# The forward loop of a recurrent attention kernel: unit work moved between the projections and the waits of the chain

## The chip, the cores and the metric

The kernel runs on one core of one Trainium2 chip. The metric is the device time of a whole execution in microseconds (us). The kernel before takes 5009.69 us (median of three runs, 5001.88 to 5017.44).

## The reference

A layer with a memory-augmented recurrent attention (A) and a gated feed-forward (B) is run forward and backward. The outputs are the layer's result and nine gradients, in bf16. Only the forward recurrence matters here:

```python
for s in range(n_seg):                       # 64 segments of 32 tokens
    xs = x[:, s * seg_len:(s + 1) * seg_len, :].copy()
    h = jnp.concatenate([mem, xs], axis=1)   # 8 memory rows + 32 tokens, 640 wide
    q = jnp.einsum('btd,dhe->bhte', h, Wq)   # 32 heads of 128
    k = jnp.einsum('btd,dhe->bhte', h, Wk)
    v = jnp.einsum('btd,dhe->bhte', h, Wv)
    scores = jnp.einsum('bhqe,bhke->bhqk', q, k) * scale
    scores = jnp.where(mask[None, None], scores, -1000000000.0)
    p = _softmax(scores, axis=-1)
    o = jnp.einsum('bhqk,bhke->bhqe', p, v)
    o = jnp.einsum('bhte,hed->btd', o, Wo)
    mem = o[:, :M, :].copy()                 # the next segment's memory
    outs.append(o[:, M:, :])
```

## The kernel before, in words

The program is a row of phases on one core. The function `recurrence` (phase 3) is the forward loop; `chain(t, gap)` writes one step of it, for t from 0 to 63. A step has two kinds of work.

The chain is what the next step needs: the eight memory rows. With `hx` (memory rows and the rows of tokens that ride along, turned) it projects K, Q and V in halves of 512 columns (`half` and `packed_half`, L306), turns the memory rows' keys and queries by a product with a selection matrix (L314), copies them out (L521 into `kT`, L530 into `qmT`), and puts the memory rows of V into `vt` by eight small VectorE copies (L539). Then come the scores of the memory rows (L544, copied to `sTm` at L546), a transpose (L554), the softmax (maximum L556, subtraction L558, exp L560, sum L562, reciprocal L564, scaling L566 into `Pm`), a transpose of `Pm` (L571) with its two ScalarE copies into `PTm` (L574), the product with `vt` (L580) and two VectorE copies into `oTm` (L582, L583), the output projection (`packed_out`, L325), the fold of its two halves (`fold_add`: ScalarE copy L334 into `fup`, VectorE sums L336 into `fsum`), the fold's turn (L352), and the cast into the next `hx` (L597).

The unit work is the attention of the tokens. Three segments are one tile `tl`, and a unit is four heads (of eight groups, `qd`) of a tile. In step t the units of the tile before are handled: three when t mod 3 is 0 or 1, two when it is 2. A unit goes through these functions: `ld` (loads of q or v, SP queue), `turn_q` (four transposes L632, ScalarE copy L634), `scores` (L644 to L649), `soft` (VectorE maximum L658 and scaling L660; four ScalarE exps L664 with their sums), `norm` (VectorE reciprocal L674, GpSimd multiply L675, store L676), `turn_p` (transposes L683, VectorE copy L684), and in the step after `pv` (products L703 and L710, ScalarE copies L705 and L712, stores L706 on ScalarE's queue and L713 on GpSimd's). Beside it, keys of the tile after next are loaded (`ld_k`) and turned (`kprep`, L615, ScalarE copy L617). `ride` (L495) and `oride` (L694) are GpSimd copies that put token rows into `hx` and `oTm`.

What is put where is written out by hand: `chain` calls `gap(name)` at nine places (W0, W1, W2 among the projections; G1 after `sTm`; G2 after `Pm`; G3 after `PTm`; G4 before the output projection; G5 after the fold's sums; G6 after `hx`), and `FILL` lists the unit functions of each. After the filling, `gap` adds one or two matmuls that nobody reads (`WARM`, L734) in G2 to G5. At the end `in_order` (L275) ties each instruction to the one written before it on its engine, so every engine runs its instructions in the order of the text; a waiting instruction holds all behind it on its engine. The unit work's tiles in PSUM share one tag of five banks, the chain has three banks of its own (`bA`, `bB`, `bC`).

Of the kernel before, what the change touches and what calls it, by code (L numbers as in the profile page):

```python
# [16 lines left out]
P = 128  # L17
# [356 lines left out]
def phase3_Afwd(k, W4, Wv, Wk_):  # L374
    nc, tc = k.nc, k.tc
    D, DC, S, H, HD, T = k.D, k.DC, k.S, k.H, k.HD, k.T
    Wq = W4.tile([P, DC, HD], BF16, name="Wq", tag="w2")
    Wo = W4.tile([P, H, D], BF16, name="Wo", tag="w3")
    with tc.tile_pool(name="ast", bufs=1) as st:
        kTs = [st.tile([P, H, 120], BF16, name=f"kT{i}") for i in range(2)]  # L380

        vt = st.tile([104, HD // 2], BF16, name="vt")
        hxs = [st.tile([P, DC, 32], BF16, name=f"hx{i}") for i in range(2)]
        qTs = [st.tile([P, 4, P], BF16, name=f"xqT{i}") for i in range(2)]
        xPs = [st.tile([120, 4, P], BF16, name=f"xP{i}") for i in range(3)]
        PTs = [st.tile([120, 4, P], BF16, name=f"xPT{i}") for i in range(2)]
        oTm = st.tile([P, H, 32], BF16, name="oTm")
        first_part(k, Wv, Wk_, Wq, Wo, kTs, vt, hxs, qTs + xPs + PTs + [oTm])
        recurrence(k, Wv, Wk_, Wq, Wo, kTs, vt, hxs, qTs, xPs, PTs, oTm)
    return Wo  # L390
# [62 lines left out]
def recurrence(k, Wv, Wk_, Wq, Wo, kTs, vt, hxs, qTs, xPs, PTs, oTm):  # L453
    nc, tc = k.nc, k.tc
    D, DC, S, H, HD, T = k.D, k.DC, k.S, k.H, k.HD, k.T
    with tc.tile_pool(name="achain", bufs=1) as ch, \
# [3 lines left out]
        bA, bB, bC = [psm.tile([P, 512], F32, name=f"bank{i}") for i in range(3)]  # L460
        pm = bA
        rides = {}
        WARM = dict(G2=1, G3=1, G4=2, G5=1)

        def ride_ld(t):
            x0 = k.NB0 + 24 * t
            b, sub = t // 4, t % 4
# [29 lines left out]
        def chain(t, gap):  # L497
# [72 lines left out]
            for a in range(2):  # L570
                nc.tensor.transpose(ps3[64 * a:64 * a + 40, :], Pm[:, a, :], k.ident[:], tile_position=(0, 64 * a))  # L571
            PTm = ch.tile([104, 8, 16], BF16, name="PTm", tag="fsum")
            for a in range(2):
                nc.scalar.copy(PTm[64 * a:64 * a + 40].rearrange("p q h -> p (q h)"), ps3[64 * a:64 * a + 40])  # L574
            gap("G3")
            poms = [bview(b, P, 16, 8) for b in (bC, bB)]
            for j in range(16):
# [2 lines left out]
                    nc.tensor.matmul(poms[a][:, j, :], vt[p0:p0 + 40, j * P:(j + 1) * P], PTm[p0:p0 + 40, :, j],  # L580
                                     start=True, stop=True, tile_position=(p0, 0))
            nc.vector.tensor_copy(oTm[:, 0:16, 0:8], poms[0])  # L582
            nc.vector.tensor_copy(oTm[:, 16:32, 0:8], poms[1])  # L583
            dump(sv, k.QVS[t // 4, :, :, t % 4, 1])
            if t + 1 == T:
                gap("G4")
# [20 lines left out]
            k.load_x(kr, 0, k.x_src(tl, "k", c0, c0 + 512), nc.sync)  # L607
            uu["kr", tl, qd] = kr

        def kprep(tl, qd):  # L610
            ns, nm, nx, n = k.geo(tl)
            kr = uu.pop(("kr", tl, qd))
            pt = ps.tile([P, 4, nx], BF16, name="kpt", tag="x", bufs=5)
            for j in range(4):
                nc.tensor.transpose(pt[:, j, :], kr[0:nx, j * P:(j + 1) * P], k.ident[0:nx, 0:nx])  # L615
            dst = kTs[tl % 2][:, qd * 4:qd * 4 + 4, 0:n].rearrange("p h (s c) -> p h s c", c=40)[:, :, :, 8:40]
            nc.scalar.copy(dst, pt[:].rearrange("p h (s c) -> p h s c", c=32))  # L617

        def ld(w, tl, qd, eng=nc.sync):
            nm = k.geo(tl)[1]  # L620
# [6 lines left out]
        def turn_q(tl, qd):  # L627
            n = k.geo(tl)[3]
            r = uu.pop(("q", tl, qd))
            pt = ps.tile([P, 4, n], BF16, name="qpt", tag="x", bufs=5)  # L630
            for j in range(4):
                nc.tensor.transpose(pt[:, j, :], r[0:n, j * P:(j + 1) * P], k.ident[0:n, 0:n])  # L632
            qT = qTs[qd % 2]
            nc.scalar.copy(qT[:, :, 0:n], pt[:])  # L634

        def scores(tl, qd):
            ns, nm, nx, n = k.geo(tl)
            h0 = qd * 4
            kT = kTs[tl % 2]
            qT = qTs[qd % 2]  # L640
            mb = (k.mask3 if ns == 3 else k.mask1)[:]
            sp = ps.tile([P, 4, n], F32, name="xsp", tag="x", bufs=5)
            mb = bass.AP(tensor=mb.tensor, offset=mb.offset, ap=[list(mb.ap[0]), [0, 4], list(mb.ap[1])])
            nc.tensor.matmul(sp[:], k.ident[0:n, :], mb, start=True, stop=False, skip_group_check=True)  # L644
            for j in range(4):
                kv = kT[:, h0 + j, 0:n].rearrange("p (s c) -> p s c", c=40)
                nc.tensor.matmul(sp[:, j, nx:n], qT[:, j, :], kv[:, :, 0:8], start=False, stop=True,
                                 skip_group_check=True)
                nc.tensor.matmul(sp[:, j, 0:nx], qT[:, j, :], kv[:, :, 8:40], start=False, stop=True,  # L649
                                 skip_group_check=True)  # L650
            uu["s", tl, qd] = sp

        def soft(tl, qd):
            n = k.geo(tl)[3]
            h0 = qd * 4
            sp = uu.pop(("s", tl, qd))
            mx = fl.tile([120, 4], F32, name="xmx", tag="xmx", bufs=2)
            nc.vector.reduce_max(mx[0:n], sp[0:n], axis=AX.X)  # L658
            nmx = fl.tile([120, 4], F32, name="xnm", tag="xnm", bufs=2)
            nc.vector.tensor_scalar(nmx[0:n], mx[0:n], -k.scale, None, op0=ALU.mult)  # L660
            Pb = xPs[qd % 3]
            Z = fl.tile([120, 4], F32, name="xZ", tag="xZ", bufs=2)
            for j in range(4):
                nc.scalar.activation(Pb[0:n, j, 0:n], sp[0:n, j, :], ACT.Exp, bias=nmx[0:n, j:j + 1], scale=k.scale,  # L664
                                     accum_out=Z[0:n, j:j + 1])
            rz = fl.tile([120, 4], F32, name="xrz", tag="xrz", bufs=2)
            uu["z", tl, qd] = Z, rz

        def norm(tl, qd, eng=nc.gpsimd, q=nc.gpsimd):
            n = k.geo(tl)[3]  # L670
            h0 = qd * 4
            Pb = xPs[qd % 3]
            Z, rz = uu.pop(("z", tl, qd))
            nc.vector.reciprocal(rz[0:n], Z[0:n])  # L674
            eng.tensor_tensor(Pb[0:n, :, 0:n], Pb[0:n, :, 0:n], bc_last(rz[0:n], n), ALU.mult)  # L675
            q.dma_start(k.PR[tl][:, h0:h0 + 4, :], Pb[0:n])  # L676
# [16 lines left out]
            if 0 <= t - k.OT0 < k.NO:  # L693
                nc.gpsimd.tensor_copy(oTm[:, :, 8:32], uu.pop(("o", t))[:])  # L694

        def pv(tl, qd, q=nc.gpsimd):
            n = k.geo(tl)[3]
            c0 = qd * 512
            v = uu.pop(("v", tl, qd))
            if 4 * tl < k.NO:  # L700
                pt = ps.tile([P, 4, 96], F32, name="xot", tag="x", bufs=5)
                for j in range(4):
                    nc.tensor.matmul(pt[:, j, :], v[0:n, j * P:(j + 1) * P], PTs[qd % 2][0:n, j, 0:96], start=True, stop=True)  # L703
                ot = fl.tile([P, 4, 4, 24], BF16, name="xoT", tag="xoT", bufs=2)
                nc.scalar.copy(ot[:].rearrange("p c h t -> p h c t"), pt[:].rearrange("p h (c t) -> p h c t", t=24))  # L705
                nc.scalar.dma_start(k.OTX[4 * tl:4 * tl + 4, :, 4 * qd:4 * qd + 4, :].rearrange("c p h t -> p c (h t)"),  # L706
                                    ot[:].rearrange("p c h t -> p c (h t)"))
            po = ps.tile([P, 512], F32, name="xpo", tag="x", bufs=5)
            for j in range(4):
                nc.tensor.matmul(po[:, j * P:(j + 1) * P], PTs[qd % 2][0:n, j, :], v[0:n, j * P:(j + 1) * P],  # L710
                                 start=True, stop=True)
            nc.scalar.copy(v[0:n], po[0:n])  # L712
            q.dma_start(k.OR[120 * tl:120 * tl + n, c0:c0 + 512], v[0:n])  # L713

        start = len(nc.cur_bb.bb.instructions)
        ride_ld(0)
# [8 lines left out]
        def gap_of(t):  # L725
# [4 lines left out]

            def gap(g):
                FILL(g, t, at, kbatch)
                for i in range(WARM.get(g, 0)):
                    nc.tensor.matmul((bA if g == "G4" else bB)[:], k.ident[:], Wq[:, 0, 0:512], start=True, stop=True)  # L734
            return gap

        def FILL(g, t, at, kbatch):
            kb = kbatch.get(t, ())
            if g == "W0":
                oride_ld(t)  # L740
                at(pv, t - 1, 0)
                at(turn_p, t - 1, 2)
                for u in kb[0:2]:
                    ld_k(*u)
            elif g == "W1":
                at(pv, t - 1, 1)
            elif g == "W2":
                at(pv, t - 1, 2)
                ride_ld(t + 1)
            elif g == "G1":  # L750
                oride(t)
                at(scores, t, 0)
                at(turn_q, t, 2)
                for i in range(2):
                    at(lambda a, b: ld("q", a, b), t + 1, i)
            elif g == "G2":
                at(scores, t, 1)
                at(scores, t, 2)
                for u in kb[0:2]:
                    kprep(*u)  # L760
                for u in kb[2:]:
                    ld_k(*u)
                for i in range(3):
                    at(lambda a, b: ld("v", a, b), t, i)
            elif g == "G3":
                at(soft, t, 0)
                at(soft, t, 1)
            elif g == "G4":
                at(soft, t, 2)
                for i in range(3):  # L770
                    at(norm, t, i)
            elif g == "G5":
                at(turn_p, t, 0)
                at(turn_q, t + 1, 0)
                at(lambda a, b: ld("q", a, b), t + 1, 2)
            elif g == "G6":
                at(turn_p, t, 1)
                at(turn_q, t + 1, 1)
                for u in kb[2:]:
                    kprep(*u)  # L780
        tail = [u for t in sorted(batch) if t >= T for u in batch[t]]
        batch = {t: b for t, b in batch.items() if t < T}
        for t in range(T):
# [9 lines left out]
        ld("q", *tail[2])  # L793
        turn_q(*tail[1])
        scores(*tail[0])
        FILL("W2", T, at_end, {})
        ld("q", *tail[3])
        ld("v", *tail[0], nc.gpsimd)
        for i in range(len(tail) + 2):
# [1295 lines left out]
```

## Time and profile before

| | |
|---|---|
| median of the runs | 5009.69 us |
| the profiled execution | 4992.93 us |
| its span | 4991.2 us |
| instructions | 160105 |
| TensorE busy (matmul) | 4497.8 us, 90% |
| VectorE, ScalarE, GpSimd busy | 2211.8, 1680.4, 1969.0 us |
| granted TensorE clock, mean | 0.961 |
| the forward loop | 411 to 1705 us |

The page and the answers from the trace have one line for a group of instructions: source line, engine (PE is TensorE, PEld its weight loads, DVE VectorE, ACT ScalarE, POOL GpSimd, SP the queue that only issues transfers), operation, what is written from what, shapes and count. In a timeline a line begins with its start and its length in us, and ends in brackets with the idle time of its engine before it and what ended that. Lines with the same source line are runs of a helper, so L90 and L92 (`copy`) are told apart by the tiles they write. The matmuls' ends are modelled.

### The profile page before, as it was taken

Reading aid. Unit: us, or ns where it says so; the run is one execution under the profiler, and the core shown is the slowest. Engines: PE = TensorE matmul, PEld = TensorE weight load, DVE = VectorE, ACT = ScalarE, POOL = GpSimd, SP = SyncE. Lnnn points to the kernel's source line nnn. Section 1 sums busy time; section 2 is a strip of 40 time slices with the busy share of each in tenths; the row PEclk is TensorE's granted clock in tenths of the full one; section 3 lists DMA queues with packets and bytes.
Section 4 is the critical chain, followed back from the end, with each engine's and each line's share of the span. In section 5 each row is a group of like instructions: output and inputs, shape, how many; then the busy total and the mean of one; then the engine's idle time right before and its main releaser. Section 6 shows DMA issues by size and latency. Waiting matters only on the chain.

```text
span 4991.2 us, 160105 instructions
## 1 busy us (share of the span) xinstructions
PE 4497.8 (90%) x64274; PEld 2891.4 (58%) x64544; DVE 2211.8 (44%) x7173; ACT 1680.4 (34%) x4768; POOL 1969.0 (39%) x3320
## 2 busy tenths in 40 slices
PE   8888998988898784789999999799999999999999
PEld 4445555555555552556666665556666566667675
DVE  8624555555556522445555554322333233311361
ACT  5422555555555521233333332322233222300000
POOL 6521444444444404345544443533444333411340
PEclk9999999999999886899999999899999999999999
DMA  8653555555555488677777775843565445659783
GB/s 275 219 178 111 164 168 165 168 166 169 165 163 160 127 194 163 175 202 216 214 210 207 205 205 147 179 113 108 130 146 130 107 109 132 164 169 226 163 192 94
DMA packets 1041986, 836.04 MB, mean 168 GB/s; under 512 B 594859, under 2 KB 927391, under 8 KB 1039239
## 3 DMA queue, kind: packets, MB, share of 16 engines
q1 hardware_dynamic: 817639, 547.28, 41.4%
q0 software_dynamic: 127664, 229.32, 16.5%
q10 hardware_dynamic: 95939, 49.18, 3.9%
q8 instruction: 510, 8.36, 0.7%
q14 instruction: 234, 1.91, 0.1%
HBM read 463.32 MB, written 306.24 MB: 154 GB/s over the span
## 4 chain that ended last, share of the span: by engine, by line
PE 48%; DMA 8%; issue 4%; DVE 2%; ACT 2%; SPq 1%; POOL 1%; ACTq 0%; POOLq 0%; DVEq 0%
PE wg L1476 10%; PE gbank L325 8%; PE g L1457 7%; PE oa L1618 3%; DMA dS<-DSR 3%; PE wa L2005 2%; PE pgxb L1938 2%; PE r6p L1408 2%; PE t6g L1439 1%; PE gbank L1086 1%; PE gbank L306 1%; SPq L270 1%; PE pghb L1917 1%; PE sT L873 1%; PE w2a L1861 1%
## 5 line engine op out<-in xcount | busy, mean ns | idle before, releaser
L1476 PE MATMUL wg<-gr,hr 128*128 128x512 bf16 x2352 | 519.1, 379 | 2.5
L1457 PE MATMUL g<-w,ghacc 128*128 128x320 bf16 x3072 | 472.2, 305 | 0.8
L1476 PEld LDWEIGHTS <-hr 128*128 128x128 bf16 x2400 | 233.9, 98 | 278.9
L1457 PEld LDWEIGHTS <-ghacc 128*128 128x128 bf16 x3072 | 294.0, 100 | 110.5 <-ACT ghacc L92 2.2
L713 POOL DMA_DIRECT2D OR<-xv x163 | 93.1, 571 | 452.2 <-ACT xv L712 337.2
L306 PEld LDWEIGHTS <-hx 128*32 128x32 bf16 x7680 | 177.2, 96 | 162.5 <-issue 1.0
L90 DVE CAST wgo<-wg 128x512 bf16<-128x512 f32 x72 | 49.8, 692 | 471.2 <-PE wg L1476 462.9
L90 DVE CAST stg<-bank 128x512 bf16<-128x512 f32 x256 | 177.1, 692 | 179.8 <-PE bank L306 176.0
L92 ACT COPY ghacc<-t6g 128x768 bf16<-128x768 bf16 (+1 forms) x176 | 137.2, 780 | 350.9 <-PE t6g L1439 348.1
L664 ACT ACTIVATE xP<-xsp,xnm 120x120 bf16<-120x120 f32 (+1 forms) x704 | 240.6, 376 | 9.3 <-DVE xnm L660 5.6
L325 PEld LDWEIGHTS <-gkv 128*8 128x8 bf16 x8192 | 178.8, 87 | 83.5 <-issue 3.4
L1186 POOL DMA_DIRECT2D VTD<-gvT x176 | 129.2, 740 | 237.5 <-ACT gvT L1185 209.4
L1423 POOL DMA_DIRECT2D GSP<-grs x48 | 25.7, 547 | 476.9 <-ACT grs L1415 475.2
L675 POOL TENSOR_TENSOR xP<-xP,xrz 120x480 bf16<-120x480 bf16 x163 | 161.7, 992 | 125.2 <-ACT xP L664 88.7
L1463 DVE TENSOR_TENSOR ghacc<-ghacc,g 128x320 f32<-128x320 f32 x192 | 93.6, 487 | 223.3 <-PE g L1457 223.3
L92 ACT CAST wgo<-wg 128x512 bf16<-128x512 f32 x48 | 28.1, 586 | 479.8 <-PE wg L1476 421.4
L1215 DVE SCALAR_TENSOR_TENSOR gdS<-gdp,Dx,gPr 120x120 bf16<-120x120 f32 (+1 forms) x680 | 183.0, 332 | 0.0
L306 PE MATMUL gbank<-WoT,gox 128*32 128x512 bf16 x2560 | 154.1, 388 | 19.6 <-POOL gox L1005 13.5
L325 PE MATMUL bank<-Wo,oTm 128*32 128x320 bf16 x4032 | 171.5, 322 | 0.1
L539 DVE COPY vt<-stg 8x512 bf16<-8x512 bf16 x512 | 160.9, 314 | 21.8 <-ACT stg L92 13.9
L325 PE MATMUL gbank<-WvT,gkv 128*8 128x320 bf16 x4096 | 169.5, 309 | 0.0
L1233 POOL DMA_DIRECT2D GXP<-gks x157 | 91.5, 583 | 192.9 <-ACT gks L1231 190.3
(343 smaller groups left out, 10817.2 us busy)
## 6 DMA issues: line engine op xcount, KB each, us to landing
QVS<-stg SPq DMA_DIRECT2D x128, 256.0 KB
vTt<-VTD SPq DMA_DIRECT2D x64, 320.0 KB
VTD<-gvT POOLq DMA_DIRECT2D x168, 120.0 KB, 4.0
DSR<-gdS POOLq DMA_DIRECT2D x168, 120.0 KB, 3.2
dS<-DSR SPq DMA_DIRECT2D x168, 120.0 KB
P<-PR SPq DMA_DIRECT2D x168, 120.0 KB
PR<-xP POOLq DMA_DIRECT2D x163, 120.0 KB, 3.2
OR<-xv POOLq DMA_DIRECT2D x163, 120.0 KB, 2.6
```

The costliest lines, as they stand in the source:

```text
L90: return nc.vector.tensor_copy(out, in_)
L92: return nc.scalar.copy(out, in_)
L306: k.nc.tensor.matmul(bank[32 * g:32 * g + 32, :], x[:, dc, :], W[:, dc, c0:c0 + 512], start=(dc == 0), stop=(dc == k.DC - 1), tile_positio ...
L325: k.nc.tensor.matmul(pm[p0:p0 + nq, 0:320], x[:, h, :], W[:, h, 320 * b:320 * b + 320], start=(first and i == 0), stop=(last and i == 15), ...
L539: nc.vector.tensor_copy(vt[p0:p0 + 8, c0:c0 + 512], sv[32 * g:32 * g + 8, b * 512:(b + 1) * 512])
L664: nc.scalar.activation(Pb[0:n, j, 0:n], sp[0:n, j, :], ACT.Exp, bias=nmx[0:n, j:j + 1], scale=k.scale, accum_out=Z[0:n, j:j + 1])
L675: eng.tensor_tensor(Pb[0:n, :, 0:n], Pb[0:n, :, 0:n], bc_last(rz[0:n], n), ALU.mult)
L1186: nc.gpsimd.dma_start(k.VTD[tl][:, :, h0:h0 + 4, :], vTq[:])
L1215: nc.vector.scalar_tensor_tensor(dS[0:n, j, 0:n], dp[0:n, j, :], Dx[0:n, j:j + 1], Pr[0:n, j, 0:n], op0=ALU.subtract, op1=ALU.mult)
L1457: nc.tensor.matmul(pg[:], ring[:, i, j, r0:r0 + P], Ws[qd][i][:, j, 320 * h:320 * h + 320], start=(i == 0 and j == 0), stop=(i == 2 and j ...
L1476: nc.tensor.matmul(pw[:], hr[:, tl, dc * P:(dc + 1) * P], grs[i][:, tl, :], start=(tl == 0), stop=(tl == NF - 1))
L1618: nc.tensor.matmul(ac[j][i][:], orr[:, w, jj * P:(jj + 1) * P], gow[:, w, 320 * i:320 * i + 320], start=(w == 0), stop=(w == NW - 1))
```

## The change

Only `recurrence` and the list of its buffers change. The diff, shortened where code only moves:

```diff
-        qTs = [st.tile([P, 4, P], BF16, name=f"xqT{i}") for i in range(2)]
+        qTs = [st.tile([P, 4, P], BF16, name=f"xqT{i}") for i in range(3)]
...
-        WARM = dict(G2=1, G3=1, G4=2, G5=1)
...
-            for a in range(2):
-                nc.scalar.copy(PTm[64 * a:64 * a + 40].rearrange("p q h -> p (q h)"), ps3[64 * a:64 * a + 40])
+            nc.scalar.copy(PTm[:].rearrange("p q h -> p (q h)"), ps3)
...
-            nc.vector.tensor_copy(oTm[:, 16:32, 0:8], poms[1])
+            nc.scalar.copy(oTm[:, 16:32, 0:8], poms[1])
...
+        def soft_max(tl, qd, sub=False):
+            n = k.geo(tl)[3]
+            sp = uu["s", tl, qd]
+            mx = fl.tile([120, 4], F32, name="xmx", tag="xmx", bufs=1)
+            nc.vector.reduce_max(mx[0:n], sp[0:n], axis=AX.X)
+            if sub:
+                nc.vector.tensor_tensor(sp[0:n], sp[0:n], bc_last(mx[0:n], n), ALU.subtract)
+                nmx = None
+            else:
+                nmx = fl.tile([120, 4], F32, name="xnm", tag="xnm", bufs=2)
+                nc.vector.tensor_scalar(nmx[0:n], mx[0:n], -k.scale, None, op0=ALU.mult)
+            Z = fl.tile([120, 4], F32, name="xZ", tag="xZ", bufs=3)
+            uu["m", tl, qd] = nmx, Z
+        def soft_exp(tl, qd, j0=0, j1=4):
+            n = k.geo(tl)[3]
+            sp, (nmx, Z), Pb = uu["s", tl, qd], uu["m", tl, qd], xPs[qd % 3]
+            if nmx is None:
+                nc.scalar.activation(Pb[0:n, :, 0:n], sp[0:n], ACT.Exp, scale=k.scale)
+                uu["zs", tl, qd] = Pb
+            else:
+                for j in range(j0, j1):
+                    nc.scalar.activation(Pb[0:n, j, 0:n], sp[0:n, j, :], ACT.Exp, bias=nmx[0:n, j:j + 1], scale=k.scale,
+                                         accum_out=Z[0:n, j:j + 1])
...
         def norm(tl, qd, eng=nc.gpsimd, q=nc.gpsimd):
...
+            if uu.pop(("zs", tl, qd), None) is not None:
+                nc.vector.tensor_reduce(Z[0:n], Pb[0:n, :, 0:n], axis=AX.X, op=ALU.add)
             nc.vector.reciprocal(rz[0:n], Z[0:n])
...
             gap("W0"):
                 at(pv, t - 1, 0)
-                at(turn_p, t - 1, 2)
+                at(turn_q, t, 1)
             W1:
                 at(pv, t - 1, 1)
+                at(turn_p, t - 1, 2)
+                at(lambda a, b: ld("v", a, b), t - 1, 2)
             W2:
-                at(pv, t - 1, 2)
             G1:
-                at(scores, t, 0)
+                at(pv_mm, t - 1, 2)
                 at(turn_q, t, 2)
+                at(lambda a, b: pv_turned(a, b, qo=nc.gpsimd), t - 1, 2)
             G2:
-                at(scores, t, 1)
-                at(scores, t, 2)
-                for u in kb[0:2]:
-                    kprep(*u)
-                for u in kb[2:]:
-                    ld_k(*u)
-                for i in range(3):
+                at(pv_rows, t - 1, 2)
+                for i in range(3):
+                    at(scores, t, i)
+                at(soft_max, t, 0)
+                for i in range(2):
                     at(lambda a, b: ld("v", a, b), t, i)
             G3:
-                at(soft, t, 0)
-                at(soft, t, 1)
+                at(lambda a, b: soft_exp(a, b, 0, 2), t, 0)
+                at(soft_max, t, 1)
             G4:
-                at(soft, t, 2)
-                for i in range(3):
-                    at(norm, t, i)
+                at(lambda a, b: soft_exp(a, b, 2, 4), t, 0)
+                at(lambda a, b: soft_max(a, b, True), t, 2)
+                for u in kb[0:2]:
+                    kprep(*u, 'v')
+                for u in kb[2:]:
+                    ld_k(*u)
+                at(norm, t, 0)
+                at(soft_exp, t, 1)
+                at(norm, t, 1)
+                at(soft_exp, t, 2)
             G6:
                 at(turn_p, t, 1)
-                at(turn_q, t + 1, 1)
                 for u in kb[2:]:
                     kprep(*u)
+                at(norm, t, 2)
```

`pv` is split into `pv_mm` (the products L703 and L710), `pv_turned` (copy L705 and store L706, for the third unit on GpSimd's queue) and `pv_rows` (copy L712 and store L713). The third unit's three parts now stand in G1, G1 and G2 of the step after; units 0 and 1 keep theirs in W0 and W1. `soft` is split into the maximum and the exps. For the third unit the maximum is subtracted from the scores in PSUM, one exp takes all four heads, and VectorE sums the exps afterwards. The two keys of G4 are copied by VectorE instead of ScalarE (L617 before). The five matmuls of `WARM` are gone. There is a third buffer for turned queries, since unit 1 is now turned in W0 of its own step.

## The prediction

> **What bounds the kernel now.** I read the busy times by stretch first. The loop that is edited runs from 411 to 1705 us, 1294 of the span's 4991.2 us, and nothing outside it changes.
>
> ```profile
> 411.00:1705.00 1294.00, 1160.34 (x22187) 720.48 (x22311) 738.65 (x2179) 694.46 (x2340) 544.09 (x850) 0.98 0.55 160
> ```
>
> The columns are TensorE, weight loads, VectorE, ScalarE, GpSimd, then granted clock. TensorE is busy 90%, but in parts with different limits. The cast L597 that ends a step starts 63 times from 434.2 to 1690.6 us: 20.26 us a step. Second, the waits inside the loop (who, total us, times, longest): TensorE stands still at the same four links of the recurrent chain in every step.
>
> ```profile
> PE bank L571 <- DVE Pm L566: 47.3, 64, 2.4
> PE bank L352 <- DVE fsum L336: 46.8, 63, 1.2
> PE bank L580 <- ACT PTm L574: 20.6, 58, 0.4
> PE bank L554 <- ACT sTm L546: 13.2, 31, 1.8
> ```
>
> So a step has a half bound by TensorE (projections, from the first L306 to L544) and a half bound by the chain. Third, the timeline of single steps. I call a step A, B or C by t mod 3 = 0, 1, 2: A and B handle three units, C two, and A has no third unit left over from the step before. In an A step Pm starts at 1161.3:
>
> ```profile
> 1164.50 0.17 DVE L674 RECIPROCAL xrz<-xZ 120x4 f32<-120x4 f32 x1
> 1164.92 0.98 POOL L675 TENSOR_TENSOR xP<-xP,xrz 120x480 bf16<-120x480 bf16 x1 [2.48 <-ACT xP L664]
> 1166.19 0.59 POOL L676 DMA_DIRECT2D PR<-xP  x1 [0.30 <-POOL xP L675]
> 1166.80 1.00 POOL L675 TENSOR_TENSOR xP<-xP,xrz 120x480 bf16<-120x480 bf16 x1
> 1168.31 0.38 PE L683 MATMUL xpp<-ident,xP 120*128 120x120 bf16 x4
> 1169.01 0.83 PE L306 MATMUL bank<-Wk,hx 128*32 128x512 bf16 x12
> ```
>
> GpSimd's second multiply ends at 1167.80; L683, which needs it, runs 0.5 us later, held by the chain. The next step's projections start 7.7 us after Pm. Fourth, VectorE's eight copies into vt, in that A step and in the next, a B step:
>
> ```profile
> 1156.57 3.40 DVE L539 COPY vt<-stg 8x512 bf16<-8x512 bf16 x8
> 1156.98 0.29 POOL L495 COPY hx<-ride 128x120 bf16<-128x120 bf16 x1
> 1157.21 0.83 POOL L694 COPY oTm<-oride 128x768 bf16<-128x768 bf16 x1
> 1177.24 1.18 DVE L539 COPY vt<-stg 8x512 bf16<-8x512 bf16 x4
> 1178.60 1.17 DVE L539 COPY vt<-stg 8x512 bf16<-8x512 bf16 x4 [0.19 <-ACT stg L92]
> ```
>
> In the B step GpSimd's copies come at 1181.05, after the copies of vt; in the A step they fall among them, and one vt copy (0.28 us otherwise, longest 1.38) stands until they are over. Fifth, equal stretches of 3.41 us, with the clock:
>
> ```profile
> 1015.14:1018.55 3.41, 1.78 (x26) 1.20 (x27) 2.08 (x8) 2.06 (x8) 2.90 (x6) 1.00 0.61 154
> 1018.55:1021.96 3.41, 3.41 (x66) 1.78 (x69) 1.36 (x6) 2.81 (x16) 1.59 (x3) 0.50 0.77 228
> 953.70:957.11 3.41, 1.83 (x32) 1.31 (x35) 2.20 (x8) 2.06 (x8) 3.01 (x6) 1.00 0.61 155
> 957.11:960.52 3.41, 3.41 (x66) 1.74 (x65) 1.24 (x6) 2.69 (x16) 1.59 (x3) 0.50 0.77 233
> 1103.88:1107.30 3.42, 2.14 (x36) 1.61 (x29) 1.58 (x7) 2.23 (x10) 2.80 (x5) 1.00 0.72 223
> ```
>
> After 1.78 or 1.83 us of TensorE work the next stretch has half the clock; after 2.14 it has not. Over the loop the drops follow stretches of up to 2.2 us, and none under 1.93 went without one. I take 2.05 as the border. There are ten drops in the 57 full steps (6 to 62), each after a stretch that begins 0.9 to 2.2 us before Pm; they lengthen L325 from 2.46 to 3.28 us and a step by about 0.8.
>
> [...] here stretches of 2.14 us, half of it transposes, kept the clock, so I count them. [...]
>
> **The change, part by part.** Times below count from the first projection (K) or from Pm.
>
> Projections. The third unit's L703/L710 leave W2: 0.5 us of TensorE in B and C (L544 starts 9.35 after K in B, 8.64 in A; 0.22 of that is a turn_p). turn_q of unit 1 enters W0 (+0.22), turn_p of unit 2 goes from W0 to W1 (0). L544 starts 0.27 sooner in B and C, 0.22 later in A. Leaving G6, turn_q frees 0.17 only where nothing else holds K.
>
> Up to Pm. In B and C sTm no longer stands behind two ScalarE copies (about 0.6 us), but two unit transposes and products now stand before L554, so sT to mmx is some 1.3 against 1.4. What decides is vt: GpSimd's hx and oride copies stood behind the OR store of the third unit (waits on ScalarE's xv, 11.8 us into the step). That store moves to G2, so the copies start at 8.65 after K in every step, as in A now. A vt copy then stands until 9.85, six more take 0.295 each: vt ends at 11.6, mmx starts at 11.7. Before: 11.7 in B and C. So Pm stays at 13.0 in B and C; in A it goes from 12.8 to 13.0. Where the ride load delays hx (one step in four) B and C gain 0.4, so 0.1 each on average. Sum for A, B, C: 0.2 - 0.1 - 0.1 = 0.
>
> Pm to L325. One PTm copy instead of two saves 0.26, one oTm copy moves to ScalarE and saves 0.2, but VectorE has two maxima and two scalings (1.6 us) ahead of its oTm copy, and with one xmx buffer each waits for the one before. L325 starts 2.07 after Pm against 2.33: 0.26 gained. The five L734 matmuls (0.38 to 0.63 us each) cost nothing now: in undisturbed steps L325 starts at the end of the oTm copy.
>
> L325 to the next K, A and B. ScalarE's exps end about when L325 does, so fup starts 0.5 earlier. But VectorE now has ahead of the first reciprocal: maximum 0.65, the new subtraction, two kT copies of 0.36 (L428, the same form). No row has the subtraction; bounds are 0.49 (L1463, 128x320) and 0.69 (a cast of 512); [...] the ends shift K by -0.17 or +0.03. The reciprocal comes at 3.9 after Pm (3.2 now), multiply 4.3 to 5.3, store issued by 6.2, second multiply 6.2 to 7.2, L683 at 7.45, K at 7.9 against 7.7. L683 stands ahead of K in TensorE's order, so hx, ready at 6.7, waits. A and B lose 0.25 each. C has no third unit, no subtraction: K at 6.7 against 6.95, gains 0.27. Sum: +0.2 us per three steps. The third unit's sum of exps and scaling in G6 (0.65 and 0.18 on VectorE) lie beside K's first half (1.26) and cost nothing; without that cover a stg cast would be late by 0.8. Its OTX store goes from ScalarE's queue (0.39) to GpSimd's (about 0.55), ahead of QM, QVM and PM: GpSimd is free again 1.9 after Pm, 2.4 before its first multiply. The loads that move behind vt (kr) or into W1 (xv) have 3 us or more of cover on SP's queue, with landings near 2.3 us.
>
> The clock. Counting TensorE's work in 3.41 us: in C, from the end of two scores (1.15 before Pm) there are L571 0.23, L580 0.59, kprep 0.5 and the start of L325, 1.5 to 1.6 us; the stretch stays under 2.05 for beginnings over 2.4 us, so it drops in 70% of C steps. A likewise, 64%. B holds 2.2, and keeps. New is the wait between L325's end (4.5) and K (7.9) in A and B: turn_p, turn_q, fold, turn_p, kprep make 1.7; under 2.05 for beginnings over 1.35 us, 40% of steps. Cost: in C L325 at half clock, between 0.8 (as now) and 1.67 (a step at 448 us had 4.13), say 1.3; in A that is hidden by GpSimd's later multiply, 0.1; after the new wait K's 2.5 us run at half clock: 0.8 to 1.7, say 1.45. Per three steps: 0.7 x 1.3 + 0.64 x 0.1 + 2 x 0.38 x 1.45 = 2.1, less today's 0.4: +1.7.
>
> **Sum.** +1.9 us per three steps, 13 triples up to step 45: 25 us. Later steps, without L703, have less on ScalarE; I take two thirds, 6 triples: 7 us. Light steps before the units: 0. So +32 us: the profiled execution, 4992.9 (span 4991.2), would become 5025, the median 5009.7, which is 17 above it, 5042.
>
> **Rivals.** (1) The clock drops no oftener than now: since three steps (61.3 us) nearly fill 18 windows (61.4), drops only come when the steps drift into them. Then +0.2 x 19 = 4 us: 5014. For it: ten drops in 57 steps now; against: five L734 matmuls a step leave. (2) Faster: GpSimd's copies miss the vt copies, and the multiplies come before hx. Then Pm is 0.4 to 0.7 earlier and K 0.7 to 0.9 earlier in A and B: up to 3.2 per three steps, -60 us; half of it, 4980, is what I would expect. It decides if hx starts later than 10.0 after K, and the first reciprocal before 3.2 after Pm. Against it: the order on both queues. (3) Slower still: both half-clock stretches in nearly every step, +70, 5080.
>
> **Numbers.** Forecast 0.58, rival 1 0.19, rival 2 0.17, rival 3 0.06. About 0.3%, 15 us, is what a measurement here can tell from no change. Faster 0.17, same 0.19, slower 0.64. The range reaches from half of rival 2's gain to rival 3: 4992 to 5085.
>
> **What would show it.** vt groups of 3.4 us in B and C; the first reciprocal (L691 there) 3.9 after Pm and the turn of xP (L700 there) ahead of K with no other work; stretches at 0.50 beginning at K in A and B and at L325 in C; loop clock below 0.95. It is wrong if the loop's clock stays at 0.98, or if mmx comes before 11.2 in B and C.

## The result and the profile after

The kernel after takes 5051.39 us, median of four runs (5040.09 to 5058.85), beside 5006.85 for the kernel before (four runs; the 5009.69 above is the median of three of them): ratio 1.0084, 95% interval 1.0057 to 1.0111. The profiled execution took 5047.45 us (span 5045.7) against 4992.93. The loop, from the first hx cast to the last, went from 1256.3 to 1321.6 us, 65.2 more; the rest of the program, untouched, from 3734.9 to 3724.2. Over the 14 profiled executions of this study, all of different kernels, the rest lies between 3708 and 3744, so its 11 can't be told from no effect.

The busy times of the loop's stretch of the kernel after, with the columns of the prediction (TensorE, weight loads, VectorE, ScalarE, GpSimd, granted clock):

```profile
411.00:1770.30 1359.30, 1200.66 (x21992) 737.02 (x21990) 823.27 (x2281) 604.28 (x1933) 566.44 (x878) 0.90 0.52 152
```

The clock in the loop fell from 0.98 to 0.90. TensorE's busy times (1160.34 before, 1200.66 after) can't be compared as they stand: the trace of the kernel before lacks the records of 127 of its 320 cover matmuls (the ones of L734 that nobody reads), though it has their weight loads:

```profile
L734 PEld LDWEIGHTS <-ident x320: 95/98/117, 423.8 to 1707.4; 128*128 128x128 bf16 x160
L734 PE MATMUL bank<-Wq,ident x193: 379/389/634, 426.6 to 1707.4; 128*128 128x512 bf16 x193
```

The missing ones are those of G2, in the wait for Pm, and of G5, ahead of the fold's turn. Put back at their weight loads, 0.39 us each where nothing else runs, they add some 24 us to the 1160 (an estimate), so of the 40 us that TensorE seems busy longer 16 are left, with fewer matmuls. The waits of TensorE at the four links of the chain, in the same stretch (us in total, times, longest):

```profile
PE bank L569 <- DVE Pm L564: 64.4, 64, 3.1
PE bank L577 <- ACT PTm L571: 24.4, 59, 0.4
PE bank L352 <- DVE fsum L336: 21.1, 52, 0.9
PE bank L325 <- DVE oTm L579: 15.9, 41, 0.6
```

The wait for Pm grew from 47.3 to 64.4, the one for the fold fell from 46.8 to 21.1; both numbers of before hold some 12 us in which the unrecorded matmuls ran, by the same estimate. Ahead of L325 there is a wait that the cover had filled before. An A step of the kernel after, in which Pm starts at 938.09:

```profile
940.49 3.95 PE L325 MATMUL bank<-Wo,oTm 128*32 128x320 bf16 x64 [0.42 <-DVE oTm L579]
942.04 0.17 DVE L691 RECIPROCAL xrz<-xZ 120x4 f32<-120x4 f32 x1
944.24 1.00 POOL L692 TENSOR_TENSOR xP<-xP,xrz 120x480 bf16<-120x480 bf16 x1
946.08 0.38 PE L700 MATMUL xpp<-ident,xP 120*128 120x120 bf16 x4
946.19 0.20 DVE L594 CAST hx<-bank 128x40 bf16<-128x40 f32 x1 [0.33 <-PE bank L352]
946.57 2.34 PE L306 MATMUL bank<-Wk,hx 128*32 128x512 bf16 x40
```

GpSimd's second multiply is done at 945.24. It is not what holds the next step: L325 takes 3.95 us instead of 2.46, so hx is late. VectorE's vt copies in the B step that follows, with GpSimd's copies:

```profile
954.88 3.21 DVE L537 COPY vt<-stg 8x512 bf16<-8x512 bf16 x8
955.10 0.30 POOL L493 COPY hx<-ride 128x120 bf16<-128x120 bf16 x1
955.33 0.83 POOL L711 COPY oTm<-oride 128x768 bf16<-128x768 bf16 x1
```

They now meet in B steps too (2.27 us for the eight copies before). Last, stretches of 3.41 us: the one ahead of a drop and the one after, for that A step and that B step (in both traces every change of the granted clock in the loop lies on one grid of this length):

```profile
936.96:940.37 3.41, 1.41 (x47) 1.05 (x43) 2.80 (x11) 1.65 (x9) 0.58 (x1) 1.00 0.57 175
940.37:943.78 3.41, 3.29 (x52) 2.28 (x56) 1.98 (x6) 2.37 (x13) 1.13 (x2) 0.50 0.55 154
957.44:960.85 3.41, 2.24 (x62) 1.74 (x61) 2.77 (x11) 2.12 (x7) 2.28 (x4) 1.00 0.36 89
960.85:964.26 3.41, 3.35 (x59) 2.34 (x55) 2.78 (x9) 3.21 (x18) 1.34 (x3) 0.50 0.86 248
```

The half-clock stretch lies under L325 both times. The loop before had 14 such stretches (47.8 us), the loop after 76 (259.4 us) in 62 steps, most often one every six stretches (20.5 us), about the length of a step. L325 shows it in the sum over all steps; the line of before stands first, then that of after:

```profile
L325 PE MATMUL bank<-Wo,oTm 128*32 128x320 bf16 x4032 | 171.5, 322 | 0.1
L325 PE MATMUL bank<-Wo,oTm 128*32 128x320 bf16 x4032 | 237.7, 416 | 17.7 <-DVE oTm L579 15.9
```

### The profile page after: what moved, and what is told of

Its sections match the earlier page's. It is cut to its first block, busy times and chain, and to the rows that moved or that the text cites. A ratio compares the mean times of both kernels' runs of the same rounds, so it can differ in the third digit from the quotient of the medians.

```text
span 5045.7 us, 159510 instructions
## 1 busy us (share of the span) xinstructions
PE 4548.0 (90%) x64224; PEld 2902.5 (58%) x64224; DVE 2296.0 (46%) x7276; ACT 1589.8 (32%) x4355; POOL 1991.7 (39%) x3349
## 3 DMA queue, kind: packets, MB, share of 16 engines
q14 instruction: 232, 1.89, 0.1%
## 5 line engine op out<-in xcount | busy, mean ns | idle before, releaser
L306 PEld LDWEIGHTS <-hx 128*32 128x32 bf16 x7680 | 181.5, 98 | 175.6 <-issue 21.4
L325 PE MATMUL bank<-Wo,oTm 128*32 128x320 bf16 x4032 | 237.7, 416 | 17.7 <-DVE oTm L579 15.9
L325 PEld LDWEIGHTS <-gkv 128*8 128x8 bf16 x8192 | 178.4, 87 | 82.7 <-issue 3.9
L325 PEld LDWEIGHTS <-oTm 128*32 128x32 bf16 x4032 | 155.4, 130 | 84.7 <-issue 24.5
L672 ACT ACTIVATE xP<-xsp,xnm 120x120 bf16<-120x120 f32 (+1 forms) x540 | 186.5, 373 | 21.6 <-DVE xnm L660 18.7
L537 DVE COPY vt<-stg 8x512 bf16<-8x512 bf16 x512 | 182.1, 356 | 16.6 <-ACT stg L92 9.7
L325 PE MATMUL gbank<-WvT,gkv 128*8 128x320 bf16 x4096 | 168.8, 308 | 0.0
L306 PE MATMUL gbank<-WoT,gox 128*32 128x512 bf16 x2560 | 151.9, 383 | 17.8 <-POOL gox L1042 11.7
```

Of the source, the lines that this page charges most:

```text
L306: k.nc.tensor.matmul(bank[32 * g:32 * g + 32, :], x[:, dc, :], W[:, dc, c0:c0 + 512], start=(dc == 0), stop=(dc == k.DC - 1), tile_positio ...
L325: k.nc.tensor.matmul(pm[p0:p0 + nq, 0:320], x[:, h, :], W[:, h, 320 * b:320 * b + 320], start=(first and i == 0), stop=(last and i == 15), ...
L537: nc.vector.tensor_copy(vt[p0:p0 + 8, c0:c0 + 512], sv[32 * g:32 * g + 8, b * 512:(b + 1) * 512])
```

## The experiments

Theory: the lost cover lets the clock drop in each step, and that is most of the loss. Rivals: the moved work itself costs, by GpSimd's copies against vt, by the late multiplies, or by a load. "A+B+C" in the table is the length of three steps, from the first L306 of a step to that of the next, means over steps 7 to 45. Each ratio is to the kernel before on the same chip. All added matmuls write what nobody reads; no run leaves out a part of the computation.

| kernel | time, us | ratio, 95% interval | loop, us | half-clock stretches | A+B+C, us |
|---|---|---|---|---|---|
| before | 5006.85 | 1 | 1256.3 | 14 | 61.5 |
| after | 5051.39 | 1.0084, 1.0057 to 1.0111 | 1321.6 | 76 | 64.9 |
| 1 after, WARM back | 5018.42 | 1.0042, 1.0027 to 1.0057 | 1289.0 | 35 | 63.9 |
| 2 before, no WARM | 5046.78 | 1.0103, 1.0082 to 1.0124 | 1312.6 | 68 | 64.5 |
| 3 after, rides late | 5050.95 | 1.0104, 1.0082 to 1.0126 | 1334.5 | 73 | 65.0 |
| 4 after, norm first | 5037.78 | 1.0073, 1.0056 to 1.0091 | 1312.5 | 72 | 64.5 |
| 5 after, full cover | 4997.46 | 1.0002, 0.9990 to 1.0014 | 1258.2 | 4 | 62.4 |
| 6 cover, rides and norm first | 4983.10 | 0.9965, 0.9952 to 0.9977 | 1254.0 | 10 | 61.4 |
| 7 before, more cover | 4985.12 | 0.9968, 0.9953 to 0.9983 | 1249.8 | 4 | 61.0 |
| 8 before, chain copies | 5126.14 | 1.0250, 1.0230 to 1.0270 | 1391.9 | 56 | 68.7 |
| 9 cover, key load early | 4990.35 | 0.9978, 0.9966 to 0.9991 | 1245.0 | 8 | 61.4 |
| 10 all mended | 4949.56 | 0.9898, 0.9882 to 0.9915 | 1208.7 | 3 | 59.0 |
| 11 before, cover, one PTm copy | 4977.74 | 0.9957, 0.9941 to 0.9973 | 1236.1 | 1 | 60.7 |
| 12 mended, no cover | 5001.71 | 0.9993, 0.9981 to 1.0004 | 1269.6 | 51 | 61.5 |

**1, the cover back; 2, the cover taken from before.** In the kernel after:

```diff
+        WARM = dict(G2=1, G3=1, G4=2, G5=1)
...
                 FILL(g, t, at, kbatch)
+                for i in range(WARM.get(g, 0)):
+                    nc.tensor.matmul((bA if g == "G4" else bB)[:], k.ident[:], Wq[:, 0, 0:512], start=True, stop=True)
```

and in the kernel before:

```diff
-        WARM = dict(G2=1, G3=1, G4=2, G5=1)
+        WARM = dict()
```

> The changed kernel with one part undone: the five matmuls that nobody reads are back in G2 to G5. Theory (the clock): the 61 half-clock stretches of the changed kernel's loop fall to fewer than 20, L325 goes back from 3.8 us to about 2.5 and most of the loss goes: about 5012 us, since the two matmuls in G4 now delay L325 by some 0.4 us in C steps. Rival (the queues: the late reciprocal on VectorE, the multiplies on GpSimd and the vt copies cost the time, and the clock only follows): the time stays near 5045 us or rises by the matmuls' own time.

> The kernel before with one part of the change alone: the five matmuls that nobody reads are taken out. Theory (the clock): about one half-clock stretch in a step, as in the changed kernel; loop longer by 0.4 to 0.8 us a step, 5030 to 5055 us in all. Rival (the queues): the matmuls stood in idle time, so nothing changes or a few us are gained, 4995 to 5010 us.

Taking five matmuls a step from the kernel before and nothing else makes 68 half-clock stretches and the whole loss. Giving them back to the kernel after removes 41 of 76 stretches and half the loss, less than expected. (The 61 of the expectation are drops in the 57 full steps, of whatever length; the table counts stretches of 3.41 us in the whole loop.) The two parts (56 in the loop from removing the cover, 33 from all the rest with cover) are more than the 65 together, and so are the stretches that they add (54 and 21, against 62 together). Theory right in the main; something else remains.

**3, GpSimd's ride copies later.** `ride(t + 1)` and `oride(t)` are issued behind the store of Pm:

```diff
-            if t + 1 < T:
-                ride(t + 1)
             gap("G1")
...
             nc.gpsimd.dma_start(k.PM[t].rearrange("p (a c) -> p a c", a=2), Pm[:])
+            if t + 1 < T:
+                ride(t + 1)
+            oride(t)
```

> The changed kernel with GpSimd's two copies (hx and oTm from the ride tiles) issued after the store of Pm, so that they don't meet VectorE's vt copies. Both theories expect vt groups of 1.2 us again and the maximum mmx at 11.0 to 11.2 us into a step. Theory (the clock sets the step, which lasts six windows of 3.41 us): the gain is mostly taken by the half-clock stretches, 5030 to 5050 us. Rival (queues): Pm comes 0.4 to 0.7 us sooner in each of 57 steps and the time falls by 20 to 35 us, to 5010 to 5030 us.

vt is free (2.3 us for eight copies in every step, Pm 12.2 to 12.3 after the first L306 in A and C), yet nothing is gained. The timeline of an A step of this kernel shows the first reason:

```profile
939.17 1.36 DVE L661 TENSOR_SCALAR xnm<-xmx 120x4 f32<-120x4 f32 x1
939.44 0.30 POOL L493 COPY hx<-ride 128x120 bf16<-128x120 bf16 x1
939.67 0.84 POOL L712 COPY oTm<-oride 128x768 bf16<-128x768 bf16 x1
```

A scaling of four columns, 0.17 us otherwise, lasts 1.36, until GpSimd's copies are over (940.53 against 940.51); it stands ahead of the oTm copy, so L325 starts 3.5 after Pm in A, not 2.4. The collision was moved, not removed. By the records, which are rough for GpSimd, VectorE's scaling starts 0.27 us ahead of GpSimd's first copy and is the one that stands, as in all 30 such cases of this run; its 120 scalings take 547 ns on average. With 73 half-clock stretches the clock is as low as before (0.91 in the loop), so how much of the 0.8 it would have taken by itself can't be read here.

**4, the first normalization ahead of the kprep copies.** In G4:

```diff
+                at(norm, t, 0)
                 for u in kb[0:2]:
                     kprep(*u, 'v')
-                at(norm, t, 0)
```

> The changed kernel with the first unit's reciprocal and GpSimd multiply written ahead of the two kT copies on VectorE. Both theories expect the reciprocal 0.7 us sooner after Pm. Theory (the clock): L325 at half clock ends about when the second multiply did, so under 0.15 us a step is gained: 5040 to 5055 us. Rival (queues): the next projections start 0.7 us sooner in two of three steps, 38 steps: 5015 to 5030 us.

The first reciprocal comes 3.4 after Pm instead of 3.9 in A and B. Three steps are 0.4 shorter, and the ratio's interval overlaps that of the kernel after; the time lies between the two ranges, nearer to the theory's. The late multiply costs little here: 72 half-clock stretches are left, and where L325 takes 3.95, as in the A step of the kernel after shown above, hx is later still (its cast starts at 946.19, the multiply ends at 945.24).

**5, full cover.** Matmuls of 512 columns at all places where TensorE stands beside a wait:

```diff
+        PRE = dict(G5=(2, 2, 0), G6=(2, 2, 1))
+        END = dict(G2=(5, 3, 5), G3=(1, 1, 1), G4=(1, 1, 1), G5=(1, 1, 2))
...
             def gap(g):
+                for i in range(PRE.get(g, (0, 0, 0))[t % 3]):
+                    nc.tensor.matmul((bA if g == "G4" else bB)[:], k.ident[:], Wq[:, 0, 0:512], start=True, stop=True)
                 FILL(g, t, at, kbatch)
+                for i in range(END.get(g, (0, 0, 0))[t % 3]):
+                    nc.tensor.matmul((bA if g == "G4" else bB)[:], k.ident[:], Wq[:, 0, 0:512], start=True, stop=True)
```

> The kernel after, with 512-column matmuls that nobody reads put wherever its trace shows TensorE idle beside a wait: behind the scores 5, 3 and 5 of them in steps A, B and C, one behind the PTm transposes, one ahead of L325, and 2 + 2 ahead of the turns that wait for GpSimd's multiplies. All of the change's moves stay. Theory (the loss is the clock): the half-speed stretches of the loop fall from 76 to under 15, mid-loop steps take about 20.5 (A), 20.6 (B) and 20.6 (C), and the time comes to 4985 to 5010, about that of before. Rival (the moves themselves cost, above all the late multiplies that hold K): few half-speed stretches too, but steps of 21 and more, and 5020 to 5045.

The loop of this kernel:

```profile
440.31:1698.50 1258.19, 1201.67 (x21991) 707.46 (x22114) 806.40 (x2230) 593.62 (x1907) 559.25 (x868) 0.99 0.54 161
```

63 us of loop go with no step of the change undone, and the ratio is 1.0002: nearly all of the loss is the clock (experiment 7 says how much is not). But C steps end 21.8 after B steps where 20.6 was expected. In the loop of this kernel TensorE's matmuls wait 10.9 us ahead of L615 (the third unit's kprep) for kr's load. That wait is in the kernel after too, 8.8 us; in the kernel before there was none. (The 25 in the expectation of experiment 9 also adds the waits of the weight loads, which stand at the same time.) At the end of a B step of the kernel after:

```profile
1158.74 0.38 SPq L265 DMA_DIRECT2D kr<-KS  x1
...
1160.74 0.20 DVE L594 CAST hx<-bank 128x40 bf16<-128x40 f32 x1 [0.33 <-PE bank L352]
1161.65 0.34 PE L612 MATMUL kpt<-ident,kr 96*128 96x96 bf16 x4 [0.63 <-DMA kr<-KS]
1161.92 4.03 PE L306 MATMUL bank<-Wk,hx 128*32 128x512 bf16 x40
```

The load is issued 2.0 ahead of hx, since it moved with the first two kpreps to G4, behind the vt loads (one of which held the queue 2.23 us here), and lands 2.9 after its issue. The projections stand behind kprep, and their first 40 matmuls then take 4.03 at half clock (40 take 2.34 in the A step above). The four half-clock stretches left in experiment 5 are three drops, one of them two stretches long; they begin 2.2 to 2.8 after the end of hx's cast, ahead of the three C steps that stand longest in this wait (1.5 to 2.6 us).

**6, early rides.** Experiment 5, and GpSimd's copies at the start of W0 in place of where they stood, with experiment 4's edit:

```diff
             if g == "W0":
-                oride_ld(t)
+                if t < T:
+                    oride_ld(t)
+                    oride(t)
+                if t + 1 < T:
+                    ride(t + 1)
...
-                ride_ld(t + 1)
+                ride_ld(t + 2)
```

> The same cover, and besides GpSimd's two ride copies issued at the start of the step (so that they meet VectorE's PSUM copies and not its vt copies), and the first normalization ahead of the two kprep copies. If the three costs that I found (clock, GpSimd against the vt copies, first reciprocal late) are separate and add up, Pm comes 0.8 sooner in each step and K 0.3 to 0.5 sooner after Pm: 0.8 x 62 + 0.3 x 62 = 68 less than the kernel with cover alone, as far as TensorE and DMA follow: 4920 to 4960. Rival (TensorE's own work, or the clock again, takes the place of what is removed): within 15 of the kernel with cover alone.

Pm comes 0.5 to 0.8 sooner (12.2 in A, 12.4 in B), but only 4 us of loop are gained, 14 by the whole time (4997 to 4983), as the rival said. One reason is the cover itself: the five matmuls behind the scores now end after Pm, and in A the PTm copy, which started 0.39 after Pm's end in experiment 5, starts 0.96 after it. The other is kr: TensorE's matmuls now wait 30 us for it in the loop, since all but the load is earlier. A miss; experiments 9 and 10 remove the two causes.

**7, more cover for the kernel before.**

```diff
-        WARM = dict(G2=1, G3=1, G4=2, G5=1)
+        WARM = dict(G1=(0, 1, 1), G2=(4, 1, 3), G3=(1, 1, 1), G4=(2, 2, 2), G5=(1, 1, 1))
```

> The kernel before, with 3 more idle matmuls behind the scores in step A and 2 more in C, and one more ahead of the ps2 transposes in B and C; nothing else. Theory (clock): the 14 half-speed stretches of its loop go, at about 1.3 each less 0.2 per step where a matmul is late: 4985 to 5000. Rival (the stretches of before are harmless, or the added matmuls cost as much): within 0.15% of before.

As expected: 4 stretches instead of 14, 6.5 us of loop; by the whole time 0.3%. This is also the kernel to hold experiment 5 against: both have the full clock, and the loop with the change is still 8.5 us longer (1258.2 against 1249.8). So of the 65 us some 57 are the clock, and the rest is moved work: kr's load costs 13 by experiment 9, other moves gain some of it back.

**8, the change's chain copies alone.** In the kernel before, with its cover:

```diff
-            for a in range(2):
-                nc.scalar.copy(PTm[64 * a:64 * a + 40].rearrange("p q h -> p (q h)"), ps3[64 * a:64 * a + 40])
+            nc.scalar.copy(PTm[:].rearrange("p q h -> p (q h)"), ps3)
...
-            nc.vector.tensor_copy(oTm[:, 16:32, 0:8], poms[1])
+            nc.scalar.copy(oTm[:, 16:32, 0:8], poms[1])
```

> The kernel before with the change's shorter chain copies alone: one PTm copy of 104 partitions in place of two, and the second oTm copy on ScalarE beside the first on VectorE. Cover and order of the units stay. L325 should start 0.2 to 0.5 sooner after Pm; if the step is as long as its chain, 62 x 0.2 to 0.5 = 12 to 31 less: 4970 to 4990. Rival (K waits for the last turn behind GpSimd's multiplies, not for L325, or ScalarE's queue takes it back): within 0.2% of before.

Both sides missed: 125 us slower. ScalarE and the rest of L325 in a step of this kernel:

```profile
1176.95 0.30 ACT L582 CAST oTm<-bank 128x128 bf16<-128x128 f32 x1
1177.31 4.02 PE L325 MATMUL bank<-Wo,oTm 128*32 128x320 bf16 x62 [1.80 <-ACT oTm L582]
```

In the old order eight exps with their sums stand on ScalarE ahead of this copy; VectorE's half was ready at 1175.05, and L325 did two matmuls and stood for 1.8 us, which also brought a half-clock stretch in most steps (56 in the loop, 14 in the kernel before). The copy on ScalarE can't do without the moved exps: in the kernel after just two stand ahead of it and it starts 1.8 after Pm.

**9, the key load early.** Experiment 5, and in part the old place: the first kprep and the third unit's load stand in G2, ahead of the first maximum (and two cover matmuls fewer there):

```diff
             elif g == "G2":
...
+                for u in kb[0:1]:
+                    kprep(*u, 'v')
+                for u in kb[2:]:
+                    ld_k(*u)
                 at(soft_max, t, 0)
...
-                for u in kb[0:2]:
+                for u in kb[1:2]:
                     kprep(*u, 'v')
-                for u in kb[2:]:
-                    ld_k(*u)
```

> The kernel after with the full cover of the first cover run, and one step of the change taken back in part: the first kprep stands before the first maximum again, so that the third unit's key load (which needs its buffer) is issued before the v loads and not behind load_v; two cover matmuls fewer behind the scores for its transposes. In the cover run the first L306 of C steps stood 1.3 after the hx cast against 0.2, and TensorE waited there for the load of kr, 25 in the loop. If that wait is a cost of its own, C steps come to 20.8 to 21.0, the loop to 1235 to 1242, the time to 4973 to 4985. Rival (the third kprep waits as long for its turn_p and GpSimd's multiply, or the clock takes it): within 0.15% of the cover run, 4990 to 5003.

No wait for kr is left, C steps come to 20.7, about as expected, and the loop is 13 us shorter. But the loop (1235 to 1242 expected) and the time (4973 to 4985) stay above their ranges. By the whole time it lies at the edge of what the rival expected, 4990, and the intervals of 5 and 9 just meet, so it is the steps and the loop that show the gain.

**10, all mended.** Experiment 9 with the edits of 6, and G2=(0, 0, 2) in END.

> The same, and GpSimd's ride copies at the start of the step and the first normalization ahead of the other kprep copy, with less cover behind the scores (none in A and B, two in C), where the run with early rides had its PTm transposes 0.3 to 0.6 behind Pm by the cover itself. If the costs add up: A and B 19.0 to 19.6, C 20.3 to 20.8, 62 steps some 45 to 60 less than the cover run: 4935 to 4960. Rival (the clock: with the chain shorter the cover misses its places and TensorE falls to half speed again, or projections and DMA bound the step): 4970 to 4990.

It beats both kernels, 1.0% under the one before. Its loop:

```profile
437.03:1645.72 1208.69, 1128.81 (x21766) 698.17 (x21889) 765.58 (x2230) 593.56 (x1907) 556.97 (x868) 1.00 0.57 167
```

The clock is full, L325 takes 2.36, the eight vt copies 2.3, and no step waits for kr.

**11, experiment 7 and the one PTm copy of experiment 8.**

> The kernel before with the fuller cover of its own run and the one PTm copy of 104 partitions in place of two of 40, the second oTm copy left on VectorE. In the run with both chain copies the oTm copy on ScalarE stood behind the units' exponentials, L325's second half started at 4.0 after Pm, and the time rose by 125; this copy alone has no queue to stand in. If the chain sets the step, L325 starts 0.2 sooner, 62 x 0.2 = 12 under the fuller cover alone: 4965 to 4978. Rival (ScalarE's exponentials start sooner and nothing else): 4980 to 4990.

L325 starts 2.12 after Pm, not 2.33; three steps are 0.40 shorter and the loop 13.6. This part of the change is a gain in the loop; by the whole time the intervals of 7 and 11 overlap (0.9968 and 0.9957).

**12, experiment 10 without any cover.**

> The kernel that beat both, with all its cover matmuls taken out: the kernel after plus early rides, early key load and the first normalization ahead of the other kprep copy, which together were worth 36 of loop time (49 by the whole) against the cover run. Theory (without cover the clock takes back what the chain gains, as it did when only one of these was made): 60 and more half-speed stretches in the loop, 5010 to 5045, not under the kernel before. Rival (the three edits are worth the same with or without cover): 5051 less 49, that is about 5000, and 4990 to 5008.

Here my theory fell: the rival's 4990 to 5008 holds. The three mended things are worth 50 us without cover (5051 to 5002) and 48 with it (4997 to 4950, where there is also less cover behind the scores). The clock does not take back all that the chain gains. It is a cost of its own: 51 stretches, A+B+C 2.5 longer than in 10, as 5 and the kernel after differ by 2.5.

## Why the prediction was right, by its steps

The time (5042 forecast, 5051 measured) and the cause held. The sizes held less well, and that the times lie so close is in part luck: the profiled execution rose by 54.5, not 32, while 17 us were added for the median above it, where in the kernel after the median is 4 above. By three mid-loop steps the loss is 3.4, not 1.9. Experiments 5 and 7, both with the full clock, split it: the clock is 2.5 in the kernel after less 0.5 in the one before, 2.0 against 1.7 forecast; the rest is 1.4 (62.4 against 61.0) against 0.2. So the clock was sized about right, and what was put too low is the moved work, 1.0 of it kr's load. K is the first L306 as there, and the values below are medians over steps 7 to 45.

- **Projections.** L544 starts 8.85 after K in A and 9.06 in B and C; forecast 8.86 and 9.08. Right.
- **Up to Pm.** vt ends 11.65 (A) and 11.53 (B) after K, mmx at 11.68 and 11.56, Pm at 13.00 and 12.88: as forecast (11.6, 11.7, 13.0). C was missed: Pm at 13.34. Experiment 10 gives the price of the collision: Pm at 12.16 to 12.38 without it.
- **Pm to L325.** Mis-sized: 2.36 to 2.40, not 2.07, so no gain where 0.26 was counted. VectorE's maxima and scalings run without a break from Pm to the oTm copy, which starts 1.96 after Pm.
- **L325 to the next K, without the clock.** The subtraction takes 0.666 us (mean of 40), between the bounds of 0.49 and 0.69 and near the upper one; the value taken between them was the author's estimate. The first reciprocal comes at 3.96 and 3.91 (forecast 3.9), the second multiply ends at 7.15 (7.2). In experiment 5, with cover, K in A comes at 7.69 after Pm (7.9), in C at 6.91 (6.7), in B only at 8.13 (7.9), where it waits for kr.
- **"The loads that move behind vt (kr) ... have 3 us or more of cover".** Wrong for kr: the ten times that TensorE stands for it in the kernel after, it was issued 0.5 to 3.6 ahead of hx (7.2 in the mid-loop B steps of the kernel before) and landed 2.6 to 4.8 after its issue. It costs 1.0 in three steps (62.4 against 61.4 in experiments 5 and 9), part of it by the half-clock stretches that follow.
- **The clock.** The cause held, 76 half-clock stretches against 14: what experiment 5 removes is 2.5 in three steps, against 2.1 forecast. Its parts are off, so that the sum is near is luck too. Over steps 1 to 62, L325 met half clock in 19 of 20 A steps, not 64%, in all 21 C steps, not 70%, and in 16 of 21 B steps, which should have kept. The border of 2.05 failed: in the kernel before, of 59 stretches with 2.0 to 2.6 us of TensorE work 3 were followed by a drop; in the kernel after, of 38 such 28 were. One reason lies in the trace of before, which lacks two cover matmuls a step: with them put back as above, an estimate, 8 of 58 such stretches were followed by a drop, and none under 2.12 kept. That narrows the difference to the kernel after, where none under 2.31 kept, and doesn't close it. "In A that is hidden by GpSimd's later multiply, 0.1": it is 0.8 (K at 8.51 against 7.69), since hx itself is only ready at 8.33. In C L325 takes 4.03 instead of 2.36, the upper end of the bounds; the ten drops of the kernel before had lengthened it to 3.28 to 4.13, and 3.28 was the least of them. The new wait between L325 and K brought 11 drops at K after 42 A and B steps, not 40%; nine of the 11 come where TensorE stands for kr.
- **The sum over the loop.** Mid-loop 13 triples of 3.4 are 44 (25 forecast). Later steps lose 3.0 in three, nearly as much, where two thirds were taken: 17 (7 forecast). The first six, counted at nothing, lost 0.7 each: 4. Together 65.
- **Rivals.** Rival 1 (no oftener) and 2 (faster) fell by the 76 stretches and by mmx at 11.6; 3 (half clock at both places in nearly every step) by the 11 drops at K. Three steps of the kernel before are 61.5 by its trace, not 61.3, so just over 18 stretches (61.4). The range's ends do not quite follow from its terms: half of rival 2's expected gain gives 4995, not 4992, and rival 3 is 5080, not 5085. Experiment 10 reaches what rival 2 was about, with other places for the same copies.

What stays open is what sets the clock. TensorE's recorded busy time in a stretch does not separate drops from kept stretches between 2.0 and 2.6 us, and where cover matmuls lack their records the busy time is itself too low. Those that kept in the kernel after held much of L325 (0.99 us on average, against 0.24 in those that dropped). No run here isolates a kind of matmul.

## What to carry to other kernels

An idle matmul that looks like waste may be what holds the clock (five a step taken out in experiment 2: 68 half-clock stretches, not 14). Before removing it, count TensorE's work in each stretch around every wait, and take one near the border (here 1.9 to 2.6 of 3.41 us) as a possible drop; count the weight loads too, since matmul records can be missing (here 127 of 320). When work moves along a queue, follow its loads and its engine's neighbours too: here one load behind two others cost 1.0 us in three steps, and when GpSimd's copies were moved off VectorE's vt copies they stopped a scaling instead (1.36 us, not 0.17). A shorter copy on another engine is worth only as much as the order ahead of it there allows (experiment 8: 125 us slower behind eight exps).

## What was not expected of the hardware

- GpSimd's copies stop VectorE's SBUF copies (a vt copy: 283 ns alone, up to 1381 beside them in the kernel before), its scalings (0.17 us alone, 1.36 beside them in experiment 3), and its product of two SBUF tiles (`Pm`: 242 ns alone, up to 691 beside them in the kernel before), but not every SBUF instruction: the sum `Zm` takes 236 ns and the reciprocal `rZm` 166 there, beside them and alone. Nor do they stop its casts from PSUM. In experiment 10 they run beside the stg casts, which keep 692 ns, as in the kernel after, while the vt copies fall from 358 to 286 ns on average.
- Short idle gaps are enough for a half-clock stretch in nearly every step (76 in 62 steps of the kernel after). No wait of TensorE in its loop spans a whole stretch of 3.41 us: the longest is 1.89 us, and in the A stretch shown above 1.28, but the work in it adds up to 1.41 of 3.41.
- The half clock can hold for two stretches (6.83 us): in 7 of the 21 C steps of the kernel after, in one A step and at the end of one B step.
